# One written-out list of operations in a searched order, and query decays made once for both blocks

## The chip, the cores and the metric

The kernel runs on one core of one Trainium2 chip. The time is the device time of one execution in microseconds; lower is better. A profiled execution gives a trace beside it, whose span reaches from the first to the last instruction of the core. The engines are named as in the profile: PE (matrix products), PEld (its weight loads), DVE (vector), ACT (scalar activations), POOL (GpSimd) and SP, which here only issues transfers. Transfers are issued by SP, ACT and POOL and are called by the queue that issued them.

## What is computed

A decayed linear attention over `q`, `k`, `v` of 4 batches, 8 heads, 768 positions and 64 channels, and on its output a two-layer network with a leaky step:

```python
for b in range(nb):                       # blocks of the sequence
    intra = (qb @ kb.T * Dmask) @ vb      # Dmask = lam ** (i - j) below the diagonal
    inter = (qb * lam_pow) @ kv_state     # lam_pow = lam ** (i + 1)
    out[block] = intra + inter
    kv_state = lam ** block * kv_state + (kb * rev_pow).T @ vb
x = out as 3072 rows of 512
h = x @ w_in                              # 512 x 2048
g = max(h, 0) + alpha * min(h, 0)
result = g @ w_out                        # 2048 x 512
```

## The kernel before

The sequence is handled in blocks of 128, two of them (256 positions) at a time. The work is cut into 24 **units**; a unit is a chunk `c` of 0 to 5, one of two batches `bi` and one half `hh` of the heads. Four units give the 512 rows of one chunk, on which the network then runs.

For a unit `n` the steps are these. `load` and `load16` bring q, k, v; `load` uses SP and keeps 32 bits, `load16` uses POOL and casts to 16 bits in the transfer. `cast` (L268) copies q or k to 16 bits on the engine that its last argument names (A is ACT, V is DVE, G is POOL). `turn` (L288) transposes with PE into the PSUM bank "tk" and `turned` copies the result out; from unit 8 on `turn_by_dma` (L306) does the same with a transfer from SP. `key_decayed` (L278) and `decayed` (L315) multiply k and q by their decays. `cluster(old, new)` (L330) issues PE's products: first those of the old unit with the state (L346), then the scores of the new one (L364), the old unit's scores times v (L376) and the new unit's keys times v (L393). `masked` (L402) multiplies the scores by the decay mask on DVE, `state` (L419) advances the state `R`, `spread` (L439) copies it into the block-diagonal tile `RD`, and `out_of` (L407) copies the unit's output to `xT`.

For chunk `c` the network has 16 slices `f`. `up(c, f, bi, slot)` (L454) makes one 128 by 512 product in four matmuls, or half of it when `bi` is given, in the PSUM bank `slot`. `below` (L467) is ACT's relu of the negative, `gate` (L478) joins it on DVE into `g`. `down(c, t, part)` (L487) multiplies `g` by a quarter of `w_out`, `store` (L507) writes the rows out. For chunks 3 to 5 the second product is made by `product` (L582) in seven products instead of eight, from sums of blocks of `g` and `w_out` (`gate_sum`, `gate_copied`, `gate_added`, `weight_sum`); `taken` (L609) takes the results and writes them out.

`load_win(i)` and `load_wout(i)` (L109, L115) bring a quarter of each weight matrix, on POOL's queue. `fill` (L238) issues matmuls that nobody reads. `hold` (L83) writes one element of a raw tile on DVE, so that the load into that tile, which SP issues, cannot start before DVE has come to this point.

Nothing reorders the operations: the kernel runs under a manual schedule. Each engine does its instructions in the order in which the code calls them and waits for semaphores in between. Up to `key_decayed(18, "G")` (L661 to L1176) the calls are written out one by one; from there on loops produce them: `weave` (L1210) deals attention steps and network steps of chunks 3 and 4 alternately, and the last loop (L1261 to L1276) does the network of chunk 5.

The places that the prediction speaks of, in the order of the calls: `hold("k", 1, 0)` and the load of k for chunk 1, first batch; `cast(4, "k", "A")` (L759); `out_of(2, "A")` (L765) and `fill(14, 0)` (L767); `hold("k", 1, 1)` (L790) and the load of k for chunk 1, second batch; `load_wout(0)` to `load_wout(3)`; then

```python
    key_decayed(6, "G")        # L839, needs k of chunk 1, second batch
    key_decayed(7, "G")        # L840
...
    cast(6, "k", "G")          # L848
...
    turn(6)                    # L858
```

Of the kernel before, what the change touches and what calls it, by code (L numbers as in the profile page):

```python
# [11 lines left out]
def kernel(  # L12
# [132 lines left out]
    pos_i = const.tile([128, 2, 2, 64], int32, name="pos_i")  # L145
    pos_f = const.tile([128, W], fp32, name="pos_f")
# [6 lines left out]
    qdecay = const.tile([128, 2, 2, 2, L], fp32, name="qdecay")  # L153
# [9 lines left out]
    def positions():  # L163
        for half in range(2):
            nc.gpsimd.iota(
                rel_i[ds(half * 64, 64)], pattern=[[1, 3], [2, 64]], base=-1, channel_multiplier=-2
            )
        for half in range(2):
            nc.gpsimd.iota(
                rev_i[ds(half * 64, 64)], pattern=[[-1, 2]], base=L - 1, channel_multiplier=-2  # L170
            )
        nc.gpsimd.iota(pos_i, pattern=[[1, 2], [0, 2], [2, 64]], base=1, channel_multiplier=0)

    def zeros():
        for t in RD.values():
            nc.vector.memset(t, 0.0)
# [5 lines left out]
    def distances():  # L182
# [3 lines left out]
        nc.vector.tensor_copy(out=pos_f, in_=pos_i.rearrange("p e h j -> p (e h j)"))  # L186
# [14 lines left out]
    def decay_mask(hp):  # L201
        for hl in range(2):
            h = 2 * hp + hl
            nc.scalar.activation(dmask[:, hl, hp], rel_f, AF.Exp, scale=loglam[:, h : h + 1])  # L204

    def causal(hh):

        for hl in range(2):
            m = dmask[:, hl, ds(2 * hh, 2)]
            nc.vector.tensor_tensor(  # L210
                out=m, in0=m, in1=keep.unsqueeze(1).to_broadcast([128, 2, 3, 64]), op=ALU.mult
            )

    def key_decay():
        for e in range(2):
            nc.scalar.activation(kdecay[:, :, e], loglam, AF.Exp, scale=rev_f[:, e : e + 1])
# [4 lines left out]
    def query_decay(hp, block):  # L221
        x = qdecay[:, hp // 2, :, hp % 2, ds(block * 64, 64)]
        f = pos_f.rearrange("p (e a j) -> p e a j", e=2, a=2)[:, :, block]
        nc.scalar.activation(x, f, AF.Exp, scale=llp[:, hp : hp + 1])
# [90 lines left out]
    def decayed(n, eng="G"):  # L315
# [3 lines left out]
        p = ds(64, 64) if c < 2 else ds(0, L)  # L319
        engine(eng).tensor_tensor(  # L320
            out=qdT[:, :, :, p],
            in0=t["qkT"][:, 0, :, :, p],
            in1=qdecay[:, hh, :, :, p],
            op=ALU.mult,
# [231 lines left out]
    def parts(c, k, h, where="q"):  # L556

        if k != 3 and (c, k) not in SUM:
# [5 lines left out]
            2: lambda: (block_of(c, 0, 0, h), x[1]),  # L564
            3: lambda: (x[3], block_of(c, 0, 0, h)),
            4: lambda: (block_of(c, 0, 1, h), x[2]),
# [92 lines left out]


    positions()  # L661
    warm_up()
    load("q", 0, 0, 0)
    identity()
    load("k", 0, 0, 0)
    hold("k", 0, 1, 0)
    load16("v", 0, 0, 0)
    distances()
    load16("q", 0, 0, 1)
    logs()  # L670
    decay_mask(0)
    cast(0, "q", "A")
    key_decay()
    query_decay(0, 0)
    decay_mask(1)
    load16("v", 0, 0, 1)
    cast(0, "k", "G")
    load_alpha()
    fill(36, 2)
    turn(0)  # L680
    zeros()
    key_decayed(0, "V")
    load16("q", 0, 1)
    turned(0, "V")
    decay_mask(3)
    load("k", 0, 0, 1)
    load16("v", 0, 1)
    load_win(0)
    state_decay()
    decay_mask(2)  # L690
    query_decay(1, 1)
    fill(15, 2)
    cluster(None, 0)
    causal(0)
    load("k", 0, 1, 0)
    state(0, 0)
    hold("k", 2, 0)
    cast(1, "q", "A")
    cast(1, "k", "V")
    fill(17)  # L700
    spread(0, 1, "V", True)
    load16("v", 1, 0)
    query_decay(0, 1)
    fill(5, 2)
    turn(1)
    causal(1)
    cast(2, "q", "G")
    masked(0, 0)
    slopes(2)
    key_decayed(1, "V")  # L710
    decayed(0, "G")
    query_decay(3, 1)
    turned(1, "A")
    load("k", 0, 1, 1)
    cast(2, "k", "A")
    hold("k", 1, 0)
    masked(0, 1)
    fill(16, 2)
    turn(2)
    cluster(0, 1, True)  # L720
    query_decay(2, 1)
    state(0, 1)
    cast(3, "k", "A")
    decayed(1, "G")
    load16("q", 1, 0)
    load_win(1)
    masked(1, 1)
    cast(3, "q", "A")
    masked(1, 0)
    turned(2, "A")  # L730
    key_decayed(3, "G")
    spread(1, 1, "A", True)
    state(1, 0)
    spread(8, 0, "G")
    out_of(0, "V")
    fill(6, 2)
    cluster(1, None)
    key_decayed(2, "V")
    decayed(2, "G")
    load16("q", 1, 1)  # L740
# [3 lines left out]
    load_win(2)  # L744
    up(0, 0, 0, 2)
    turned(3, "A")
    state(2, 0)
    spread(2, 1, "A", True)
    below(0, 0, 0)
    masked(2, 0)  # L750
    load_win(3)
    state(1, 1)
    masked(2, 1)
    decayed(3, "G")
    gate(0, 0, 0)
    cluster(2, 3, True)
    load("k", 1, 0)
    up(0, 2, 0, 2)
    cast(4, "k", "A")  # L759
    key_decayed(4, "G")  # L760
    query_decay(3, 0)
    spread(3, 1, "A", True)
    masked(3, 0)
    state(3, 0)
    out_of(2, "A")  # L765
    state(2, 1)
    fill(14, 0)  # L767
    up(0, 1, 0, 0)
    state(3, 1)
    masked(3, 1)  # L770
    up(0, 3, 0, 1)
    below(0, 3, 0)
    cast(4, "q", "V")
    cluster(3, None)
    gate(0, 3, 0)
    turn(4)
    out_of(3, "A")
    below(0, 1, 0)
    below(0, 2, 0)
    gate(0, 1, 0)  # L780
    gate(0, 2, 0)
    load16("v", 1, 1)
    up(0, 6, None, 1)
    up(0, 2, 1, 0)
    cast(5, "k", "G")
    up(0, 5, None, 2)
    turned(4, "A")
    cluster(None, 4)
    below(0, 2, 1)
    hold("k", 1, 1)  # L790
    below(0, 6, None)
    below(0, 5, None)
    state(4, 0)
    gate(0, 2, 1)
    load_wout(0)
    load("k", 1, 1)
    key_decayed(5, "G")
    gate(0, 6, None)
    load_wout(1)
    up(0, 0, 1, 0)  # L800
    up(0, 4, None, 1)
    spread(10, 0, "G")
    cast(5, "q", "G")
    gate(0, 5, None)
    below(0, 0, 1)
    below(0, 4, None)
    up(0, 8, None, 2)
    decayed(4, "G")
    masked(4, 0)
    turn(5)  # L810
    load("k", 2, 0)
    state(4, 1)
    gate(0, 0, 1)
    spread(4, 1, "G")
    cast(7, "q", "G")
    up(0, 3, 1, 0)
    below(0, 8, None)
    spread(9, 0, "G")
    gate(0, 4, None)
    turned(5, "A")  # L820
    up(0, 7, None, 1)
    gate(0, 8, None)
    masked(4, 1)
    below(0, 3, 1)
    load("q", 2, 0)
    up(0, 1, 1, 2)
    cluster(4, 5)
    gate(0, 3, 1)
    decayed(5, "V")
    hold("k", 3, 0)  # L830
    below(0, 1, 1)
    load_wout(2)
    cast(6, "q", "G")
    up(0, 9, None, 0)
    below(0, 7, None)
    gate(0, 1, 1)
    up(0, 11, None, 2)
    state(5, 0)
    key_decayed(6, "G")  # L839
    key_decayed(7, "G")  # L840
    spread(5, 1, "A")
    masked(5, 1)
    out_of(4, "A")
    gate(0, 7, None)
    below(0, 9, None)
    below(0, 11, None)
    gate(0, 9, None)
    cast(6, "k", "G")  # L848
    gate(0, 11, None)
    up(0, 14, None, 1)  # L850
    query_decay(1, 0)
    up(0, 12, None, 0)
    state(5, 1)
    up(0, 10, None, 2)
    masked(5, 0)
    cast(7, "k", "G")
    below(0, 14, None)
    turn(6)  # L858
    cast(8, "k", "G")
    gate(0, 14, None)  # L860
    below(0, 12, None)
    gate(0, 12, None)
    cluster(5, None)
    below(0, 10, None)
    gate(0, 10, None)
    up(0, 15, None, 1)
    out_of(5, "A")
    turned(6, "V")
    up(1, 0, 0, 0)
    below(0, 15, None)  # L870
    load_wout(3)
    up(0, 13, None, 2)
    below(1, 0, 0)
    gate(0, 15, None)
    spread(11, 0, "A")
    cluster(None, 6)
    down(0, 2, 0, 1)
    turn(7)
    gate(1, 0, 0)
    below(0, 13, None)  # L880
    up(1, 2, 0, 0)
    gate(0, 13, None)
    state(6, 0)
    up(1, 1, 0, 2)
    state(6, 1)
    turned(7, "A")
    decayed(6, "G")
    masked(6, 1)
    masked(6, 0)
    spread(6, 1, "G")  # L890
    down(0, 2, 1, 2)
    below(1, 2, 0)
    cluster(6, 7)
    state(7, 0)
    gate(1, 2, 0)
    below(1, 1, 0)
    cast(8, "q", "A")
    gate(1, 1, 0)
    key_decayed(8, "G")
    down(0, 1, 0, 0)  # L900
    masked(7, 1)
    down(0, 1, 1, 2)
    down(0, 0, 0, 2)
    load16("v", 2, 0)
    spread(7, 1, "V")
    cast(9, "k", "V")
    down(0, 0, 1, 1)
    down(0, 2, 2, 2)
    down(0, 0, 2, 1)
    down(0, 2, 3, 2)  # L910
    hold("k", 2, 1)
    down(0, 0, 3, 1)
    cast(9, "q", "G")
    state(7, 1)
    out_of(6, "A")
    down(0, 1, 2, 2)
    masked(7, 0)
    turn_by_dma(8)
    decayed(8, "V")
    decayed(7, "G")  # L920
    load("k", 2, 1)
    cluster(7, 8)
    store(0, 0)
    masked(8, 1)
    up(1, 3, 0, 2)
    state(8, 0)
    query_decay(2, 0)
    down(0, 1, 3, 2)
    store(0, 2)
    turn_by_dma(9)  # L930
    spread(14, 0, "G")
    masked(8, 0)
    key_decayed(9, "G")
    out_of(7, "A")
    below(1, 3, 0)
    load("q", 2, 1)
    cast(10, "k", "V")
    up(1, 4, None, 1)
    gate(1, 3, 0)
    store(0, 1)  # L940
    up(1, 5, None, 0)
    state(8, 1)
    below(1, 4, None)
    up(1, 0, 1, 2)
    spread(8, 1, "G")
    gate(1, 4, None)
    load("q", 3, 0)
    below(1, 5, None)
    below(1, 0, 1)
    load("k", 3, 0)  # L950
    gate(1, 5, None)
    load16("v", 2, 1)
    cluster(8, 9)
    up(1, 1, 1, 1)
    cast(11, "k", "A")
    up(1, 6, None, 0)
    below(1, 1, 1)
    gate(1, 0, 1)
    key_decayed(10, "G")
# [347 lines left out]
```

## Time and profile before

| what | value |
|---|---|
| median of 3 timed runs | 220.3 us (220.16 to 220.39) |
| the profiled execution's own time | 221.63 us |
| its span | 219.8 us |
| mean granted PE clock over the span | 0.983 of full |
| transfers | 33.55 MB, 153 GB/s over the span |

The profile is read in this order. The busy shares say which engine has the least air; the 40 slices say when it has none; the windows give the same for stretches of one's own choice. The chain of waits goes back from the last instruction and names at each step what released it, so it says what a microsecond is worth where. The timeline of one engine shows each instruction with the idle time ahead of it. The view of the transfers has the time from issue to landing.

### The profile page before, as it was taken

What the parts mean: (1) busy time and instruction counts of PE and PEld (TensorE: products, weight loads), DVE (VectorE), ACT (ScalarE), POOL (GpSimd) and SP (SyncE); (2) the same over time, 40 slices, a digit from 0 to 9 for tenths busy, and PEclk for the clock granted to TensorE, in tenths of its full rate; (3) what the DMA queues carried; (4) which work ended last, traced back from release to release, by engine and by line L of the source; (5) the groups of instructions that cost most, each with busy time, mean ns of one, the idle gap of its engine ahead of it and who ended that gap; (6) DMA issues with size and microseconds to landing.
All of it is one profiled execution on the core that took longest, in us unless ns stands there. A gap on an engine that the chain in (4) does not pass through costs nothing.

```text
span 219.8 us, 5672 instructions
## 1 busy us (share of the span) xinstructions
PE 203.8 (93%) x2286; PEld 125.9 (57%) x2286; DVE 151.4 (69%) x306; ACT 117.0 (53%) x231; POOL 100.0 (46%) x162
## 2 busy tenths in 40 slices
PE   4877799399999999999999999999999999999993
PEld 4765556156455455454554555457667666666882
DVE  3899378736568874777897865875855577877811
ACT  3995488445164753447574644577445634445220
POOL 8769962448143944073558346759294100000000
PEclk9999799969999999999999999999999999999999
DMA  4999999954999999649899924797664220102123
GB/s 122 223 188 236 190 195 222 258 94 59 178 287 261 207 294 221 206 60 140 176 283 213 131 62 132 190 198 208 142 119 72 75 71 3 48 20 79 48 73 121
DMA packets 66027, 33.55 MB, mean 153 GB/s; under 512 B 34496, under 2 KB 62672, under 8 KB 66000
## 3 DMA queue, kind: packets, MB, share of 16 engines
q1 hardware_dynamic: 42576, 19.67, 37.4%
q0 software_dynamic: 21520, 10.36, 36.3%
q10 hardware_dynamic: 1904, 3.16, 4.1%
q8 instruction: 18, 0.29, 0.5%
q14 instruction: 9, 0.07, 0.1%
HBM read 27.28 MB, written 6.29 MB: 153 GB/s over the span
## 4 chain that ended last, share of the span: by engine, by line
PE 76%; DMA 11%; ACT 6%; DVE 3%; POOL 1%; issue 1%; ACTq 0%; POOLq 0%
PE h_ps L459 33%; PE o_ps L493 18%; PE p_ps L600 17%; DMA kraw<-in_k_dram 9%; PE s L364 3%; PE acc L376 2%; PE acc L346 2%; DMA lam_sb<-in_lam_dram 2%; ACT dmask L204 1%; PE acc L393 1%; POOL kdec L283 1%; ACT m L470 1%; DVE g L483 1%; ACT xT L252 1%; ACT RD L252 1%
## 5 line engine op out<-in xcount | busy, mean ns | idle before, releaser
L483 DVE SCALAR_TENSOR_TENSOR g<-m,oma,h_ps 128x512 f16<-128x512 f32 (+1 forms) x104 | 71.9, 704 | 40.4 <-ACT m L470 39.2
L459 PE MATMUL h_ps<-xT,w_in_sb 128*128 128x512 f16 (+1 forms) x416 | 97.7, 370 | 0.5 <-DVE g L483 0.5
L470 ACT ACTIVATE m<-h_ps 128x512 f32<-128x512 f32 (+1 forms) x104 | 57.9, 564 | 57.4 <-PE h_ps L459 54.2
L459 PEld LDWEIGHTS <-w_in_sb 128*128 128x128 f16 x416 | 40.1, 100 | 37.9 <-issue 3.0
L493 PE MATMUL o_ps<-w_out_sb,g 128*128 128x512 f16 x192 | 47.1, 379 | 0.0
L256 POOL COPY RD<-R 64x128 f16<-64x128 f16 x54 | 17.8, 330 | 48.4 <-DVE R L430 35.0
L405 DVE TENSOR_TENSOR sm<-s,dmask 128x512 f16<-128x512 f32 x48 | 31.8, 684 | 4.1 <-PE s L364 3.9
L493 PEld LDWEIGHTS <-g 128*128 128x128 f16 x192 | 18.2, 98 | 20.2
L283 POOL TENSOR_TENSOR kdec<-kraw,kdecay 128x512 f16<-128x512 f32 x21 | 21.9, 1048 | 8.4 <-DMA kraw<-in_k_dram 7.1
L600 PEld LDWEIGHTS <-g 128*128 128x128 f16 x192 | 18.7, 98 | 5.4
L320 POOL TENSOR_TENSOR qdT<-qkT,qdecay 128x512 f16<-128x512 f16 (+1 forms) x20 | 20.3, 1013 | 1.6 <-ACT qkT L252 0.5
L252 ACT ACTIVATE xT<-acc 128x512 f16<-128x512 f32 x20 | 11.9, 596 | 10.9 <-PE acc L376 4.9
L430 DVE SCALAR_TENSOR_TENSOR R<-R,rdecay,acc 128x64 f16<-128x64 f16 x60 | 13.9, 273 | 4.0 <-ACT xT L252 4.0
L600 PEld LDWEIGHTS <-gsum 128*128 128x128 f16 x144 | 14.1, 98 | 4.2
L242 PE MATMUL op_fill<-ident 128*128 128x128 f16 x109 | 9.1, 250 | 6.5 <-POOL ident masks.py:199 2.8
L624 ACT ACTIVATE o_sb<-p_ps 128x512 f32<-128x512 f32 (+1 forms) x16 | 7.9, 491 | 10.3 <-PE p_ps L600 10.3
L513 ACT ACTIVATE o_sb<-o_ps 128x512 f32<-128x512 f32 x12 | 7.1, 595 | 9.3 <-PE o_ps L493 9.3
L242 PEld LDWEIGHTS <-ident 128*128 128x128 f16 x109 | 8.1, 114 | 6.9 <-issue 3.9
L600 PE MATMUL p_ps<-w_out_sb,g 128*128 128x256 f16 x96 | 12.0, 273 | 0.0
L600 PE MATMUL p_ps<-wsum,gsum 128*128 128x256 f16 x96 | 12.0, 273 | 0.0
L600 PE MATMUL p_ps<-wsum,g 128*128 128x256 f16 x96 | 12.0, 273 | 0.0
L102 POOL DMA_DIRECT2D vh<-in_v_dram x13 | 11.8, 909 | 0.0
(84 smaller groups left out, 193.2 us busy)
## 6 DMA issues: line engine op xcount, KB each, us to landing
kraw<-in_k_dram SPq DMA_DIRECT2D x10, 512.0 KB, 7.9
qraw<-in_q_dram SPq DMA_DIRECT2D x8, 512.0 KB, 6.7
out_dram<-o_sb ACTq DMA_DIRECT2D x12, 256.0 KB, 5.7
out_dram<-o_sb SPq DMA_DIRECT2D x24, 128.0 KB, 2.0
vh<-in_v_dram POOLq DMA_DIRECT2D x11, 256.0 KB, 7.1
w_in_sb<-in_moe_w_in_dram POOLq DMA_DIRECT2D x4, 512.0 KB, 8.9
w_out_sb<-in_moe_w_out_dram POOLq DMA_DIRECT2D x4, 512.0 KB, 11.1
gsum<-g SPq DMA_DIRECT2D x6, 256.0 KB, 2.5
```

Of the source, the lines that this page charges most:

```text
L242: nc.tensor.matmul(t[:, 0:128], lhsT=ident, rhs=ident, start=True, stop=True)
L252: nc.scalar.activation(out, in_, AF.Copy)
L256: nc.gpsimd.tensor_copy(out=out, in_=in_)
L283: engine(eng).tensor_tensor(out=kdec, in0=kr, in1=d.unsqueeze(3).to_broadcast([128, 2, 4, D]), op=ALU.mult)
L320: engine(eng).tensor_tensor(out=qdT[:, :, :, p], in0=t["qkT"][:, 0, :, :, p], in1=qdecay[:, hh, :, :, p], op=ALU.mult,)
L405: nc.vector.tensor_tensor(out=t["sm"][hl], in0=t["s"][hl], in1=mask_of(hl, units[n][2]), op=ALU.mult)
L430: nc.vector.scalar_tensor_tensor(out=then[:, hp], in0=R[b, hh, i][:, hp], scalar=rdecay[:, 2 * hh + hp : 2 * hh + hp + 1], in1=kv[:, hp], ...
L459: nc.tensor.matmul(h_ps[:, 0:n] if bi is None else h_ps[:, 0:n].rearrange("p (e j) -> p e j", e=2), lhsT=w_in_sb[:, gi, ts(f, 128)], rhs=x ...
L470: nc.scalar.activation(m[:, 0:n], HP[c, f, bi][:, 0:n], AF.Relu, scale=-1.0)
L483: nc.vector.scalar_tensor_tensor(out=g, in0=mv, scalar=oma[:, f : f + 1], in1=hv, op0=ALU.mult, op1=ALU.add)
L493: nc.tensor.matmul(O[c, t], lhsT=gated(c, f)[:, t // 2, t % 2, :], rhs=w_out_sb[:, f, :], start=(f == 0), stop=(f == NF - 1),)
L600: nc.tensor.matmul(acc, lhsT=lhsT, rhs=rhs, start=(first and j == 0), stop=(j == NJ - 1), skip_group_check=True,)
```

## The change

The list of calls is replaced from the first to the last: what the loops made is written out too, and the order of everything is new. Of PE's instructions there are as many as before (4573 with weight loads and branches), of the same kinds. The helpers change so that a call is one instruction or a few (`zeros`, `decay_mask`, `causal`, `key_decay` take the piece as an argument), `load` may also be issued by POOL (`ring=1`), and the engine of many copies is another one. The decay of the queries is the same in both blocks of 64 positions of a row of `qdecay`; it was kept twice and made by eight activations, and is now kept once, made by four, and read with a repeated index.

```diff
-    def load(x, c, bi, part=None):
+    def load(x, c, bi, part=None, ring=0):
         h0, n = (0, H) if part is None else (part * H // 2, H // 2)
-        nc.sync.dma_start(
+        (nc.sync, nc.gpsimd)[ring].dma_start(
...
-    def zeros():
-        for t in RD.values():
-            nc.vector.memset(t, 0.0)
+    def zeros(b, hh, eng="V"):
+        engine(eng).memset(RD[b, hh], 0.0)
...
-    def query_decay(hp, block):
-        x = qdecay[:, hp // 2, :, hp % 2, ds(block * 64, 64)]
-        f = pos_f.rearrange("p (e a j) -> p e a j", e=2, a=2)[:, :, block]
-        nc.scalar.activation(x, f, AF.Exp, scale=llp[:, hp : hp + 1])
+    def query_decay(hp):
+        nc.scalar.activation(
+            qdecay[:, hp // 2, :, hp % 2, :], pos_f, AF.Exp, scale=llp[:, hp : hp + 1]
+        )
...
         engine(eng).tensor_tensor(
-            out=qdT[:, :, :, p],
-            in0=t["qkT"][:, 0, :, :, p],
-            in1=qdecay[:, hh, :, :, p],
-            op=ALU.mult,
+            out=x, in0=y, in1=d.unsqueeze(2).to_broadcast([128, 4, n, 64]), op=ALU.mult
         )
```

In the list, the parts around the places named above, as they stand after the change (other calls lie between them where three points stand):

```python
    decayed(0, "V")
    key_decayed(2, "G")
    hold("k", 1, 0)
...
    load("k", 1, 0)
...
    cast(5, "k", "G")
...
    load16("q", 1, 1)
...
    cast(4, "k", "G")
    key_decayed(4, "G")
...
    key_decayed(5, "G")
    load_win(3)
    out_of(2, "A")
    fill(14, 0)
...
    cast(4, "q", "A")
...
    hold("k", 1, 1)
...
    decayed(5, "G")
...
    load_wout(0)
    up(0, 11, None, 2)
    cast(6, "q", "G")
    load_wout(1)
    cast(6, "k", "G")
...
    key_decayed(6, "G")
...
    load_wout(2)
    spread(5, 1, "G")
...
    load_wout(3)
    turn(6)
...
    key_decayed(7, "G")
```

Further on, q of chunks 3 and 4 and k of chunks 3 and 4 (six of the loads) go through POOL:

```python
    load("q", 3, 0, ring=1)
...
    cast(12, "q", "G")
...
    load("q", 4, 1, ring=1)
    load("k", 3, 1, ring=1)
    load("k", 4, 0, ring=1)
...
    load("k", 4, 1, ring=1)
...
    load("q", 4, 0, ring=1)
```

And the last lines, where before the results of the seventh product were taken right behind it for each batch:

```python
    product(5, 3, 0, None, True)
    taken(5, 3, 0)
    taken(5, 4, 1)
    taken(5, 3, 1)
```

More of the change, by code (lines that the diff above doesn't have):

```diff
@@ L721 @@
[L721 to L725, printed above, removed]
[L726 to L740 removed]
+    cluster(None, 0)
+    causal(0, 1)
+    load("k", 0, 1, 1)
+    key_decayed(1, "V")
@@ L827 @@
     cluster(4, 5)
[L828 to L831, printed above, removed]
-    load_wout(2)
[L833 to L849, printed above, removed]
+    up(0, 9, None, 0)
```

1236 lines of the change are left out of this document (771 added, 465 removed).

## The prediction

> **What bounds the kernel now.** I read the span first, then the windows of my own choice, then the chain of waits, and last the timelines around the places where the chain leaves PE.
>
> ```profile
> span 219.8 us, 5672 instructions
> ...
> 0.00:44.15 44.15, 32.49 (x513) 23.22 (x513) 31.63 (x79) 30.24 (x70) 30.77 (x54) 0.96 1.25 204
> 44.15:203.07 158.92, 158.18 (x1656) 91.17 (x1657) 112.98 (x215) 83.07 (x152) 69.23 (x109) 0.99 0.71 146
> 203.07:219.80 16.73, 13.10 (x120) 11.49 (x118) 6.74 (x13) 3.67 (x9) 0.00 (x0) 0.98 0.24 79
> ```
>
> The columns of a window are its length, the busy time of PE, PEld, DVE, ACT and POOL, the granted PE clock, the share of the transfers and GB/s. From 44.15 to 203.07 us PE is busy for 158.18 of 158.92 us: no order can take more than the 0.74 us of gaps and what the clock held back. In the first 44.15 us PE is busy for 32.49 us, and some of that is fill or half speed; there the transfers are saturated (share 1.25). The tail is PE too. So the prediction is made ahead of 44.15 us, and the rest asks only whether the new order keeps PE full.
>
> The chain of waits (start, length, what):
>
> ```profile
> 14.46 7.00 DMA kraw<-in_k_dram
> ...
> 21.56 0.63 ACT qk L252
> ...
> 23.22 0.28 ACT xT L252
> ...
> 23.55 0.96 PE op_fill L242 x14
> ...
> 24.54 1.87 PE h_ps L459 x8
> ...
> 29.07 12.25 DMA kraw<-in_k_dram
> ...
> 41.49 2.05 POOL kdec L283 x2
> 43.54 0.56 POOL qk L256
> ...
> 44.15 0.62 PE tp L295 x8
> ...
> 45.39 3.74 PE h_ps L459 x12
> ...
> 203.07 13.11 PE p_ps L600 x120
> 216.20 0.42 DVE o_sb L622
> ```
>
> It leaves PE twice for a load of k. The first one, k of chunk 1, first batch, is held until 14.46 us and lands at 21.5; ACT stands at the cast of it, and behind that in ACT's queue is the copy to `xT` that frees the bank of the next `up`. The second, k of chunk 1, second batch, is held until 29.07, lands at 41.35, and then POOL makes both decayed keys (2.05 us) ahead of the cast (0.56) that `turn(6)` needs.
>
> PE's timeline around the second gap, its line at 27.91, and the clock in four windows of 1 us:
>
> ```profile
> 27.91 2.33 PE L459 MATMUL h_ps<-xT,w_in_sb 128*128 128x512 f16 x12
> 39.00 1.89 PE L459 MATMUL h_ps<-xT,w_in_sb 128*128 128x512 f16 x8 [0.23 <-DVE g L483]
> 44.15 0.62 PE L295 MATMUL tp<-ident,qk 128*128 128x128 f16 x8 [3.26 <-POOL qk L256]
> 25.00:26.00 1.00, 1.00 (x7) 0.67 (x6) 0.22 (x1) 0.00 (x0) 0.98 (x3) 0.50 1.30 203
> ...
> 45.00:46.00 1.00, 1.00 (x18) 0.43 (x11) 0.50 (x1) 0.57 (x1) 1.00 (x2) 0.50 0.10 31
> ...
> 47.00:48.00 1.00, 1.00 (x6) 0.75 (x5) 0.12 (x1) 0.60 (x1) 0.00 (x0) 0.50 0.84 62
> ```
>
> PE ends its work at 40.89 and idles 3.26 us. After either gap the granted clock is 0.50: the twelve matmuls at 45.39 take 3.74 us, where at full clock (1.89 for eight, with 0.16 of overlap, so 0.22 each) they take 2.6.
>
> **The change part by part.** PE's order up to `turn(6)` is the old one but for swaps of neighbours, so what comes ahead of it is decided by the other queues.
>
> *Start.* `hold("k",1,0)` now comes in DVE's queue ahead of a mask and both first `masked`; counting DVE's queue through, I put it at 12.3 us (estimate). With the 7.0 us of the load it lands at 19.3. Its cast (unit 4) goes to POOL, so ACT reaches the `xT` copy without it: about 21.9, after `cluster(2,3)` at 20.5, and the first `up` behind the fill starts at 23.0, where it was 24.54. Then ACT stands at `cast(4,"q")` instead, whose q POOL issues at about 15.6 and which lands 7.4 later, at 23.0. What is late next is ACT's copy of unit 3 and the gate that frees bank 1: the first whole `up` (27.91 before) starts at about 26.0. **-1.9 us**; bounds 0 (ACT's new wait is as long as the old) and -3.3 (both waits gone).
>
> The transfers that this and the next step rest on, issue to landing, from views narrowed to one load (k at 14.46, k at 29.07, 16-bit q, q at 30.1, then the parts of `w_out` in order, the last of them alone in flight):
>
> ```profile
> kraw<-in_k_dram SPq DMA_DIRECT2D x1, 512.0 KB, 7.0
> kraw<-in_k_dram SPq DMA_DIRECT2D x1, 512.0 KB, 12.2
> qh<-in_q_dram POOLq DMA_DIRECT2D x1, 256.0 KB, 7.4
> qraw<-in_q_dram SPq DMA_DIRECT2D x1, 512.0 KB, 16.0
> w_out_sb<-in_moe_w_out_dram POOLq DMA_DIRECT2D x1, 512.0 KB, 11.4
> w_out_sb<-in_moe_w_out_dram POOLq DMA_DIRECT2D x1, 512.0 KB, 13.3
> ...
> w_out_sb<-in_moe_w_out_dram POOLq DMA_DIRECT2D x1, 512.0 KB, 5.9
> ```
>
> *The gap at 40.89.* `hold("k",1,1)` comes three DVE operations later in the list but the work ahead of it runs 1.9 us earlier, so the load starts at 29.0 as before. In flight beside it before were two parts of `w_out`; now there is the end of `w_in`, and `w_out` starts only at about 33. I take 8 us, nearer the 7.0 than the 12.2: it lands at 37. Its cast stands ahead of the decayed keys, not behind (0.56 us): 37.6. PE comes to `turn(6)` at 26.0 plus the 12.98 us that lie between 27.91 and 40.89, at 39.0. The wait is covered; **-3.26**. With 12.2 us it would be 41.8, and 2.8 of it come back.
>
> *The clock.* Without the gap the half clock from 45.0 to 48.3 goes: **-1.65**. Here the Trainium skill says more (TensorE: Matmul & The Clock Gate, section What's actually happening): a PE idle for about one window of 3.4 us falls to half clock and stays there for about as long. The second gap (3.26 idle, 3.3 at half) agrees; the first one was filled for its last microsecond (the fill at 23.55) and was halved too. By the rule alone short new waits cost only themselves; by the rows they may cost the 1.65 again. The sum takes no second halving.
>
> *w_out later.* POOL issues the first part behind `decayed(5)`, which waits for `turn(5)` and ACT's copy: about 33.2 instead of 25.0. The first `down` is due 4.05 us of PE work after `turn(6)`, at 43.05. With the 11.4 us of the row it lands at 44.6, with 5.9 at 39: **+1.0**, bounds 0 and +3.4 (13.3).
>
> *POOL's queue in the same stretch.* Durations of POOL and of what moves to DVE and off ACT:
>
> ```profile
> L283 POOL TENSOR_TENSOR kdec<-kraw,kdecay 128x512 f16<-128x512 f32 x21 | 21.9, 1048 | 8.4 <-DMA kraw<-in_k_dram 7.1
> ...
> L256 POOL COPY RD<-R 64x128 f16<-64x128 f16 x54 | 17.8, 330 | 48.4 <-DVE R L430 35.0
> ...
> L320 POOL TENSOR_TENSOR qdT<-qkT,qdecay 128x512 f16<-128x512 f16 (+1 forms) x20 | 20.3, 1013 | 1.6 <-ACT qkT L252 0.5
> ...
> L256 POOL CAST qk<-kraw 128x512 f16<-128x512 f32 x13 | 7.9, 612 | 4.9 <-ACT qk L252 3.6 <-DMA kraw<-in_k_dram 0.9
> ...
> L102 POOL DMA_DIRECT2D vh<-in_v_dram x13 | 11.8, 909 | 0.0
> L283 DVE TENSOR_TENSOR kdec<-kraw,kdecay 128x512 f16<-128x512 f32 x3 | 2.5, 847 | 0.1
> ...
> L254 DVE COPY RD<-R 64x128 f16<-64x128 f16 x4 | 1.4, 347 | 0.0
> ...
> L254 DVE CAST xT<-acc 128x512 f16<-128x512 f32 x2 | 1.4, 688 | 0.1
> L224 ACT ACTIVATE qdecay<-pos_f,llp 128x128 f32<-128x128 f32 x8 | 3.0, 391 | 0.5 <-ACT o_sb L513 0.5
> ```
>
> From the landing of k at 37 POOL has, up to `key_decayed(7)` that `cluster(6,7)` needs: three decayed keys at 1.05, five casts at 0.61, three issues at 0.91, two pairs of `RD` copies at 0.66 and one decayed q at about 0.7, 11.0 us, so 48.0. PE is there at 39.0 plus 9.24 of work and about 1 us of waits, 49; but `cast(8,"q")` in that queue waits for a load that took 16.0. **+0.5**, bounds 0 and +2.
>
> *Moved work and query decays.* DVE gets six more decayed keys, eight more pairs of `RD` copies and six more `xT` copies: 6 x 0.85 + 8 x 0.69 + 6 x 0.69 = 14.8 us. Its cover is DVE's idle time, 46 us of the 159; if that is gone at a place, PE waits up to 0.7 there. Four `qdecay` activations go (4 x 0.39 = 1.6 us of ACT); three of the eight ran after 22 us under ACT's idle, and all four kept ones run in the start: nothing. The repeated index in `decayed` is not in the trace; the decayed keys read `kdecay` in that manner at 1.05 us against 1.0 for `decayed`, so nothing, at most 0.05 each under POOL's idle.
>
> *End.* DVE takes two results behind the last product, not one, and SP's last three stores follow: 0.42 x 1 = **+0.4**, bounds 0 and +0.7.
>
> Sum: -1.9 - 3.26 - 1.65 + 1.0 + 0.5 + 0.4 = -4.9; span 219.8 to 214.9. The profiled execution's own time is 221.63, 1.33 above the median of the runs, 220.3; I take the 4.9 from the median: **215.4 us**.
>
> **The rivals.** *More is won.* If `w_out` and POOL are in time and the first half clock (24.7 to 27.5, 1.4 us) goes too: -4.9 - 1.0 - 0.5 - 1.4 = -7.8, 212.5. For it: fewer bytes are in flight beside each load that PE awaits. Against: the bytes are the same and the transfers were saturated.
>
> *The gap only moves.* The same bytes must land, and the late `w_out` takes 13.3: PE waits 3.45 at the first `down` instead of 1.0, and the clock is halved again (1.65): -4.9 + 2.45 + 1.65 = -0.8, 219.5. For it: the share of 1.25 over the whole first window. Against: the last `w_out` took 5.9 alone.
>
> *POOL blocks on its own loads: slower.*
>
> ```profile
> qraw<-in_q_dram SPq DMA_DIRECT2D x8, 512.0 KB, 6.7
> ...
> vh<-in_v_dram POOLq DMA_DIRECT2D x11, 256.0 KB, 7.1
> ```
>
> Six loads leave SP for POOL, and `cast(12,"q")` stands on POOL behind the issue of its own load with four operations between. Until it lands POOL does nothing; behind it, up to `decayed(11)`, are eight issues, four casts, two decayed keys, three decayed q's and a pair of copies: 7.3 + 2.4 + 2.1 + 3.1 + 0.7 = 15.6 us. Between `cluster(7,8)` and `cluster(11,12)` PE has 25 whole parts of 0.865, five halves and three clusters of about 1 us, 26.8 us; the load is issued some 2 us into it. Slack is 26.8 - 2 - 15.6 = 9.2 less the landing. With 6.7 or 7.1 it fits; with 16.0 PE waits 6.8: 222.2. It makes the change a loss from a landing of 14.1 on. A page of the Trainium skill, SBUF — State Buffer, section SBUF: two separate sides, speaks for this one: vector work in some modes keeps GpSimd from writing descriptors, and loads of SP are free of that. The rows of before, 909 ns for an issue, show no such delay here; no run here shows it for these loads.
>
> **How the numbers follow.** Forecast 215.4, chance 0.48; more won, 0.20; the gap moves, 0.16; POOL blocks, 0.16. The range goes from the first rival with half a microsecond to spare, 211.9, over the second, to 220.4; it leaves out the third. A measurement tells 0.2% (0.44 us) from no change: faster 0.48 + 0.20 + most of the second, 0.79; within 0.2%, 0.04; slower 0.17.
>
> **What would show it.** PE at the eight transposes of `turn(6)` near 39 us without a gap of over 1 us; no window at clock 0.50 after 30 us; the k load of 29.0 landed by 38; a wait at the first `down` of about 1 us; and from there PE over 99% busy. Wrong it is if PE idles for over 2 us between 40 and 55, or POOL has a wait of over 4 us for a load after 55 with PE waiting for `qdT`.

## The result, and the profile after

The changed kernel takes **228.15 us** (median of 4 executions, 227.53 to 229.33), beside 220.34 us of the kernel before on the same chip: 1.0349 times as long, 95% interval 1.0294 to 1.0404. The forecast was 215.4 us, the range 211.9 to 220.4: wrong, and on the wrong side. Ratios here and below leave out executions over 1.5% above the fastest of the same kernel; where these are many (e1, e6, e9, e13, e14, e16), the median and the range of all tell more than the ratio.

The profiled execution took 228.05 us. Two lines of its page, then lines of PE's timeline up to its longest wait:

```profile
span 225.8 us, 5654 instructions
...
PE 202.2 (90%) x2286; PEld 125.8 (56%) x2286; DVE 165.9 (73%) x332; ACT 108.0 (48%) x219; POOL 97.5 (43%) x150
```

```profile
26.53 2.33 PE L457 MATMUL h_ps<-xT,w_in_sb 128*128 128x512 f16 x12
...
39.23 0.61 PE L291 MATMUL tp<-ident,qk 128*128 128x128 f16 x8
...
43.43 1.03 PE L491 MATMUL o_ps<-w_out_sb,g 128*128 128x512 f16 x4
...
48.94 1.02 PE L491 MATMUL o_ps<-w_out_sb,g 128*128 128x512 f16 x4 [1.02 <-DVE g L481]
...
69.30 2.75 PE L457 MATMUL h_ps<-xT,w_in_sb 128*128 128x512 f16 x12 [1.37 <-DVE g L481]
...
77.67 0.39 PE L344 MATMUL acc<-qdT,RD 128*128 128x128 f16 x4
86.19 0.64 PE L362 MATMUL s<-qkT 64*64 64x128 f16 x16 [8.13 <-DMA qkT<-qk]
```

The first part came nearly at the forecast times: the first whole `up` at 26.53 (forecast 26.0), `turn(6)` at 39.23 with no wait, the first `down` at 43.43. In `cluster(10, 11)` PE then stands for 8.13 us, because the transpose of unit 11 has not landed. The windows around it (columns as in the prediction) show the second part of the price:

```profile
30.00:44.15 14.15, 14.15 (x184) 8.56 (x182) 12.78 (x24) 9.85 (x21) 11.35 (x20) 1.00 1.19 235
...
80.00:82.00 2.00, 0.00 (x0) 0.00 (x0) 0.00 (x0) 0.00 (x0) 0.61 (x1) 0.65 0.95 252
82.00:84.00 2.00, 0.00 (x0) 0.00 (x0) 0.00 (x0) 0.00 (x0) 0.00 (x0) 0.50 1.49 165
...
88.00:90.00 2.00, 2.00 (x8) 0.82 (x6) 2.00 (x5) 0.88 (x3) 0.25 (x1) 0.50 1.63 118
90.00:92.00 2.00, 2.00 (x9) 0.86 (x8) 1.16 (x3) 0.00 (x0) 0.91 (x2) 0.79 1.46 187
...
94.00:220.00 126.00, 126.00 (x1267) 77.91 (x1264) 97.48 (x182) 59.57 (x110) 33.83 (x51) 1.00 0.48 106
```

PE's clock falls to half in the wait and is whole again at about 90.8 (0.79 over 90 to 92). From 86.2 to 90.8 PE works at half speed: 4.6 us, 2.3 of them lost (the expectations below have 2.65, a coarser reading). 8.1 + 2.3 = 10.4, and 225.8 - 10.4 = 215.4, within half a microsecond of the forecast span of 214.9 (the terms ahead of it do not all agree, as shown below). From 94 us PE is again busy throughout.

SP's timeline in four narrow windows has the transposes of units 12, 13, 11 and 14 in the order of issue; the view of the transfers, narrowed to the third, has its time from issue to landing:

```profile
64.84 1.81 SPq L305 DMA_TRANSPOSE qkT<-qk  x1
...
68.73 1.43 SPq L305 DMA_TRANSPOSE qkT<-qk  x1
...
70.32 4.25 SPq L305 DMA_TRANSPOSE qkT<-qk  x1
...
81.22 1.31 SPq L305 DMA_TRANSPOSE qkT<-qk  x1
```

```profile
qkT<-qk SPq DMA_TRANSPOSE x1, 15.8
```

Unit 11 is needed first and is third in line. POOL's timeline shows what is issued meanwhile:

```profile
64.77 0.60 POOL L252 CAST qk<-kraw 128x512 f16<-128x512 f32 x1
...
68.03 1.04 POOL L89 DMA_DIRECT2D qraw<-in_q_dram  x1
69.07 1.78 POOL L89 DMA_DIRECT2D kraw<-in_k_dram  x2
...
71.84 0.92 POOL L89 DMA_DIRECT2D kraw<-in_k_dram  x1
...
74.38 0.89 POOL L102 DMA_DIRECT2D vh<-in_v_dram  x1
75.26 0.89 POOL L89 DMA_DIRECT2D qraw<-in_q_dram  x1
76.14 0.90 POOL L102 DMA_DIRECT2D vh<-in_v_dram  x1
...
77.64 0.88 POOL L102 DMA_DIRECT2D vh<-in_v_dram  x1
```

The cast of k for unit 11 ends at 65.4: its transpose could go then, 5 us earlier (in e1 below it goes at 65.95). And five loads of 512 KB and three of v are issued within 10 us, with the transposes in flight.

### The profile page after: what moved, and what is told of

Same layout as the page of the kernel before. It is cut to its first block, busy times and chain, and to the rows that moved or that the text cites. A ratio compares the mean times of both kernels' runs of the same rounds, so it can differ in the third digit from the quotient of the medians.

```text
span 225.8 us, 5654 instructions
## 1 busy us (share of the span) xinstructions
PE 202.2 (90%) x2286; PEld 125.8 (56%) x2286; DVE 165.9 (73%) x332; ACT 108.0 (48%) x219; POOL 97.5 (43%) x150
## 4 chain that ended last, share of the span: by engine, by line
PE 73%; DVE 9%; DMA 9%; ACT 5%; issue 2%; DVEq 0%; ACTq 0%
PE h_ps L457 32%; PE p_ps L598 16%; PE o_ps L491 16%; DMA qkT<-qk 7%; PE s L362 3%; PE acc L374 2%; DVE g L481 2%; DVE RD L250 2%; DMA lam_sb<-in_lam_dram 2%; PE acc L344 2%; PE acc L391 1%; DVE dmask L207 1%; ACT qkT L248 1%; ACT RD L248 1%; DVE sm L403 1%
## 5 line engine op out<-in xcount | busy, mean ns | idle before, releaser
L457 PE MATMUL h_ps<-xT,w_in_sb 128*128 128x512 f16 (+1 forms) x416 | 92.9, 364 | 1.7 <-DVE g L481 1.7
L481 DVE SCALAR_TENSOR_TENSOR g<-m,oma,h_ps 128x512 f16<-128x512 f32 (+1 forms) x104 | 71.1, 702 | 21.4 <-ACT m L468 20.0
L468 ACT ACTIVATE m<-h_ps 128x512 f32<-128x512 f32 (+1 forms) x104 | 56.8, 564 | 60.9 <-PE h_ps L457 59.2
L457 PEld LDWEIGHTS <-w_in_sb 128*128 128x128 f16 x416 | 39.3, 98 | 38.7 <-issue 1.9
L491 PEld LDWEIGHTS <-g 128*128 128x128 f16 x192 | 18.7, 100 | 23.1 <-issue 3.0
L598 PEld LDWEIGHTS <-g 128*128 128x128 f16 x192 | 18.8, 98 | 4.8
L252 POOL COPY RD<-R 64x128 f16<-64x128 f16 x34 | 10.1, 298 | 24.6 <-DVE R L428 18.4
L362 PE MATMUL s<-qkT 64*64 64x128 f16 x384 | 10.3, 226 | 10.9 <-DMA qkT<-qk 8.1
L279 POOL TENSOR_TENSOR kdec<-kraw,kdecay 128x512 f16<-128x512 f32 x15 | 16.2, 1085 | 0.2
L511 ACT ACTIVATE o_sb<-o_ps 128x512 f32<-128x512 f32 x12 | 7.1, 595 | 17.0 <-PE o_ps L491 16.6
L362 PEld LDWEIGHTS <-qkT 64*64 64x64 f16 x384 | 6.3, 108 | 13.7 <-DMA qkT<-qk 8.3
L248 ACT ACTIVATE xT<-acc 128x512 f16<-128x512 f32 x14 | 8.3, 596 | 11.4 <-PE acc L391 6.7
L598 PE MATMUL p_ps<-wsum,gsum 128*128 128x256 f16 x96 | 12.3, 273 | 0.0
```

Source lines behind the costliest of these rows:

```text
L248: nc.scalar.activation(out, in_, AF.Copy)
L252: nc.gpsimd.tensor_copy(out=out, in_=in_)
L279: engine(eng).tensor_tensor(out=kdec, in0=kr, in1=d.unsqueeze(3).to_broadcast([128, 2, 4, D]), op=ALU.mult)
L362: nc.tensor.matmul(s[hl][ds(a * 64, 64), hp, 1 - e, :].rearrange("p (e j) -> p e j", e=2), lhsT=t["qkT"][p, 1, e, hp, ds(a * 64, 64)], rhs ...
L457: nc.tensor.matmul(h_ps[:, 0:n] if bi is None else h_ps[:, 0:n].rearrange("p (e j) -> p e j", e=2), lhsT=w_in_sb[:, gi, ts(f, 128)], rhs=x ...
L468: nc.scalar.activation(m[:, 0:n], HP[c, f, bi][:, 0:n], AF.Relu, scale=-1.0)
```

## The experiments

"Unit 11's transpose" is `turn_by_dma(11)`, "v of chunk 3" `load16("v", 3, 0)` and `(3, 1)`.

| run | edit | median, range of all (us) | ratio to before, interval |
|---|---|---|---|
| e1 | after, unit 11's transpose first | 222.29, 217.40 to 232.99 | 0.993, 0.9885 to 0.9974 |
| e2 | after, six loads on SP | 228.77, 227.73 to 232.10 | 1.0363, 1.0312 to 1.0414 |
| e3 | after, loads of chunk 4 later | 223.77, 221.79 to 226.13 | 1.0125, 1.0072 to 1.0179 |
| e4 | start of after, rest of before | **216.85**, 216.60 to 217.15 | **0.9824**, 0.9793 to 0.9856 |
| e5 | start of before, rest of after | 234.54, 233.61 to 244.64 | 1.0607, 1.0554 to 1.0661 |
| e6 | e1 and e3 together | 224.13, 219.10 to 226.83 | 0.9974, 0.9926 to 1.0023 |
| e7 | before, gap alone | 217.36, 216.42 to 217.53 | 0.9835, 0.9802 to 0.9868 |
| e8 | before, query decays once | 221.00, 219.15 to 221.63 | 0.9994, 0.9952 to 1.0036 |
| e9 | after, transfers in before's order | 223.68, 220.22 to 227.69 | 1.0037, 0.998 to 1.0095 |
| e10 | e4, six loads on POOL | 219.31, 217.41 to 220.87 | 0.9874, 0.9818 to 0.9931 |
| e13 | e1, and v of chunk 3 first | 221.68, 217.37 to 226.78 | 0.9871, 0.9802 to 0.9941 |
| e14 | after, v of chunk 3 first | 226.99, 220.31 to 236.89 | 1.0016, 0.9966 to 1.0066 |
| e15 | e13, six loads on SP by need | 220.48, 217.54 to 222.31 | 0.9935, 0.9895 to 0.9974 |
| e16 | e13, three loads later | 224.12, 218.97 to 226.91 | none: one left |

**The halves of the list (e4, e5).** Both lists hold the same calls (the helpers of the start are those of after in both), so they can be cut at `spread(7, 1)` and joined crosswise.

> The list of the changed kernel from its first call to spread(7, 1) (about 52 us), and from there on every remaining call in the order, on the engine and on the queue of the kernel before. The prediction's sum (start 1.9, gap 3.26, clock 1.65, less 1.0 and 0.5) says 220.3 - 5.3 = 215.0 us, if the loss is all behind 52 us. Rival: the new order of the start takes something away from the rest (buffers and loads that come earlier or later), so that the loss comes with it: 220 us or more.

> The list of the kernel before up to spread(7, 1) (about 58 us), then the remaining calls in the order, on the engines and on the queues of the changed kernel. If the start's gain and the later loss are independent: 220.5 + 228.2 - 216.9 = 231.8 us, with a wait of PE of some 8 us for the transpose of unit 11. Rival (the loss comes of the earlier start, which brings the loads of weights and the later ones closer together): 220 to 223 us.

The start of after with the rest of before wins 1.8%, and its executions lie within 0.55 us; by the medians it wins 4.1 us, where its expectation had 5.3, so it is partly luck that its profiled span is 214.9 us, the span that the prediction summed. The other way round the kernel loses 6.1%, some 3 us more than the 231.8 of two independent parts; in its profile, of its longest execution (244.64), PE waits 18.75 us for unit 11's transpose, which took 26.6 to land. So the loss comes with the rest of the list and the gain with the start. The two do not quite add up, and what makes up the 3 us is not shown.

**The gain by itself (e7, e8).**

```diff
-    load_wout(0)          # ahead of load("k", 1, 1)
-    load_wout(1)
...
+    load_wout(0)
+    load_wout(1)
     load_wout(2)
...
+    cast(6, "k", "G")
     key_decayed(6, "G")
     key_decayed(7, "G")
...
-    cast(6, "k", "G")
```

> The kernel before with two edits: the first two parts of w_out are issued just ahead of the third, and the cast of k for unit 6 stands on POOL ahead of the decayed keys of 6 and 7. By the prediction's terms: the load issued at 29.07 lands at about 37 instead of 41.3, the wait of 3.26 us and the half clock behind it (1.65) go, w_out is in time because the start is not earlier: 220.5 - 4.9 = 215.6 us. Rival (the load took 12.2 us for its own place among loads that stay): it lands after 40, 1 to 2.5 us are won, 218 to 219.5 us.

> The kernel before with the decay of the queries kept once: four activations of the eight, and the repeated index in the decayed queries; the order is otherwise the old one. By the prediction nothing: 220.5 us, within 0.3. Rival: an ACT operation of 0.39 us less ahead of the first units brings the start forward, up to 0.4 us won; or the repeated index costs 0.05 us and more on each of the 23 decayed queries, 221 us.

e7 gives 0.9835, 3.6 us by the medians, of the 4.9 expected. The transfers of the window 28.5 to 29.5, and PE's timeline:

```profile
kraw<-in_k_dram SPq DMA_DIRECT2D x1, 512.0 KB, 5.5
```

```profile
40.66 0.61 PE L295 MATMUL tp<-ident,qk 128*128 128x128 f16 x8
...
44.40 1.04 PE L493 MATMUL o_ps<-w_out_sb,g 128*128 128x512 f16 x4
```

The load that took 12.2 us takes 5.5 without the two parts of `w_out` beside it; `turn(6)` is at 40.66 without a gap, and the first `down` at 44.40, where before it was at 49.53. Of the start's gain beyond the gap little is left in the end: e4 is 0.0011 below e7, within the intervals. e8 shows no effect of the part of the change that its name tells of, as forecast.

**Order or bytes (e1, e2, e3).**

```diff
+    turn_by_dma(11)       # e1
     turn_by_dma(12)
...
-    load("q", 4, 1, ring=1)    # e2: the six without ring=1
+    load("q", 4, 1)
...
     cast(14, "k", "G")
+    load("q", 4, 1, ring=1)    # e3: moved here from 68 to 78 us
+    load("k", 4, 0, ring=1)
+    load("k", 4, 1, ring=1)
+    load("q", 4, 0, ring=1)
+    load16("v", 4, 0)
```

> One transfer moves: the transpose of unit 11 stands on SP ahead of that of unit 12, not behind that of 13. Theory O (order: unit 11's transpose is issued at 70.3 us although its operands are ready at 65.4, and comes in the thick of the loads): issued at about 65.5 it lands in 5 to 6 us, by 72, the 8.13 us wait of PE at 78.06 and the half clock behind it (2.65) go, 228.15 - 10.8 = 217.4 us, or 215.5 if nothing else is late. Theory C (contention: the loads that POOL issues from 68 to 78 us slow every transpose, wherever it stands): unit 11 is out of it, but those of 12, 13 and 14 land later instead; PE gets a wait of 3 to 6 us at the scores of unit 12, 13 or 14, 221 to 225 us.

> The six loads of q and k of chunks 3 and 4 that POOL issues are issued by SP at the same places of the list; nothing else changes. Theory P (what hurts is that POOL's queue issues them): the transposes land in 3 to 5 us as in the kernel before, the 8.13 us wait goes, 216 to 219 us. Theory C (the bytes in flight hurt, whoever issues them) : the transposes of 11, 13 and 14 still take 10 us or more, or stand on SP behind loads that wait for a free buffer; the wait of PE stays at 5 to 10 us, 225 to 231 us. Theory O says the same as C here.

> Five loads (q and k of chunk 4, 512 KB each, and v of chunk 4, first batch) stand on POOL behind the cast of k for unit 14, some 10 us later; the order of the transposes on SP stays as it is in the changed kernel. Theory C: with only one load of k and two of v beside them the transposes of 13, 11 and 14 land in 4 to 6 us each; unit 11 lands by 77 us, the 8.13 us wait and its half clock go, about 217.4 us; the loads that come later cost at most a wait of 2 us behind 95 us. Theory O: unit 11 is still issued at 70 us or later behind unit 13's transpose, the wait stays at over 4 us, 223 us or more.

Each theory got half of what it asked. e1: issued at 65.95, the transpose lands in 4.4 us, the wait is gone, and the profiled execution takes 217.4 us; but six of the other eleven take 224 to 233. e3: with the old place in line but fewer loads beside it, it lands in 7.2 us and PE does not wait for it; instead POOL stands 9.32 us at a cast of q whose load it issued late, and PE 2.75 us for a decayed q. e2: on SP the loads stand in one line with the transposes, unit 11's is issued only at 77.1 and lands in 9.7 us, and PE waits 10.4.

**What comes back in e1's longer executions (two more traces of it, e11 and e12).**

> The kernel with unit 11's transpose first once more, for a trace of one of its longer executions (its times went from 217.4 to 233.0 us). If it comes out over 223 us: a wait of PE of 5 us or more, and by the theory of the bytes in flight it is for the transpose of unit 13 or 14, or for a decayed q that POOL makes behind one of them; by a theory of the order alone it would be again for unit 11. If it comes out below 221 us it tells nothing new.

> The same kernel a third time, for the same reason and with the same expectations: over 223 us with a wait of PE of 5 us or more behind the transpose of unit 13 or 14 (bytes in flight) or of unit 11 (order alone); below 221 us it tells nothing new.

e11 took 220.38 us, e12 228.72. Neither side of the expectation was right: in e12 PE waits neither for 11 nor for 13 or 14. PE's timeline, POOL's, and the landing of that load:

```profile
94.58 0.43 PE L391 MATMUL acc<-vh,kdec 64*64 64x64 f16 x16 [8.35 <-DMA vh<-in_v_dram]
```

```profile
75.23 0.89 POOL L102 DMA_DIRECT2D vh<-in_v_dram  x1
```

```profile
vh<-in_v_dram POOLq DMA_DIRECT2D x1, 256.0 KB, 19.3
```

It is v of chunk 3, issued behind four loads of q and k, three of them of chunk 4. The stretch 60 to 82 us in the shorter (profiled e1) and the longer execution (e12) of this one kernel:

```profile
60.00:82.00 22.00, 21.60 (x251) 11.76 (x249) 20.71 (x42) 11.82 (x24) 17.83 (x23) 1.00 1.17 258
```

```profile
60.00:82.00 22.00, 20.44 (x244) 11.18 (x243) 20.71 (x41) 11.68 (x24) 17.55 (x23) 1.00 1.12 190
```

The engines of the transfers are as busy (1.17 and 1.12), but they moved 258 GB/s in one and 190 in the other.

**One cure after the other (e6, e9, e13 to e16).** e6 has the edits of e1 and e3 and moves `cast(17, ...)` and `turn_by_dma(17)` behind `turn_by_dma(16)`; e9 leaves the engines in after's order and gives SP the order of before. The others, against after:

```diff
+    turn_by_dma(11)            # e13, e15, e16
     turn_by_dma(12)
...
+    load16("v", 3, 0)          # e13 to e16
+    load16("v", 3, 1)
...
     turn_by_dma(13)
+    load("q", 4, 0)            # e15: the six on SP, four of them here
+    load("k", 4, 0)
+    load("q", 4, 1)
+    load("k", 4, 1)
...
     cast(17, "k", "G")
+    load("q", 4, 1, ring=1)    # e16: moved here
+    load("k", 4, 1, ring=1)
+    load16("v", 4, 0)
```

> Both cures in the changed kernel: the transpose of unit 11 ahead of that of 12, and the five loads of chunk 4 on POOL behind the cast of k for unit 14; besides, the casts and the transpose of unit 17 stand behind the transpose of unit 16, so that POOL does not stand at a cast of 17 while its load is in flight (9.32 us with the loads later alone). Theory (order and bytes in flight together are the whole loss): no wait of PE over 1 us behind 45 us, 215 to 217.5 us, and the single executions lie within 2 us of one another. Rival (the new order of the engines has further waits of its own behind 80 us): a wait of over 2 us at another place, 219 us or more.

> The list of the changed kernel, with PE, DVE, ACT and POOL in its order, but behind spread(7, 1) SP issues the 28 loads and transposes in the order of the kernel before (the six loads of POOL among them on SP), each as early in the list as its operands allow. Theory X (only the order of the transfers costs): the wait of 8.13 us at unit 11 goes and no other comes, 216.9 us as with the first part alone, at most 218. Theory Y (the new order of the four engines behind 52 us costs by itself, because an engine's operation now stands ahead of what PE needs): a wait of over 2 us stays, 220 us or more.

> The changed kernel with two transfers moved: unit 11's transpose on SP ahead of unit 12's, and v of chunk 3 (both batches) on POOL ahead of the loads of q for chunk 4 and k for chunks 3 and 4. Theory L (the loss is just two transfers that are needed first and issued behind others needed later): no wait of PE over 1.5 us behind 45 us in any execution, 216.5 to 218 us, the single executions within 2 us of one another. Theory C (the bytes in flight slow whatever comes next): a third transfer is late, the times stay spread over 5 us or more, median 219 us or more.

> The changed kernel with v of chunk 3 on POOL ahead of the loads of q for chunk 4 and k for chunks 3 and 4; the transposes stay in their order. Theory L: unit 11's transpose is late as before, with 6 to 9 us of waiting in PE, 225 to 229 us. If the wait goes too (218 us or less), the place of the transpose on SP was not the cause, and the four loads ahead of it were.

> The changed kernel with the six loads of q and k on SP in the order of need: behind the transpose of unit 10 q of chunk 3, then the transposes of 11 and 12, k of chunk 3, the transpose of 13, and only then the four loads of chunk 4; v of chunk 3 stands on POOL where the burst began. Theory of the pace (SP issues in line, so the transposes that PE needs next are never behind six loads): no wait of PE over 1.5 us behind 45 us in any execution, 216.5 to 218 us, single executions within 2 us. Theory of the bytes alone (the same 3 MB between 63 and 82 us are in flight, whoever issues them): spread of 5 us or more, median 219 us or more.

> The changed kernel with unit 11's transpose ahead of unit 12's, v of chunk 3 ahead of the loads on POOL, and three loads (q and k of chunk 4, second batch, and v of chunk 4, first batch: 1.25 of the 3.25 MB that POOL asks for from 68 to 78 us) some 15 us later on POOL, behind the cast of k for unit 17. Theory D (density: as many bytes in that stretch as in the fast kernel, 2.25 MB from 68 to 79 us, and what is needed first issued first, are enough): 216.5 to 218.5 us, single executions within 2 us. Rival (the changed order has too little room behind 63 us for any load to be slower than usual, wherever the bytes are): a wait of over 2 us for some other transfer, median 219.5 us or more, spread over 4 us.

No edit brings the changed order to e4's time in every execution. In each profile another wait stands last: in e9 DVE at `cast(12, "k", "V")`, which its order has ahead of a gate, for a load that SP now issues later (PE 4.59 us); in e13 and e16 a stop of PE in the middle of a product (below); in e15 a decayed q (2.63 us) behind the transpose of unit 14, which SP issues only at 88.69, behind the loads; in e6 a copy to `RD` (1.67 us). e14 keeps the wait for unit 11 in its profile (2.67 us). Theory L, two misplaced transfers, fails with e13; theory D, the density, with e16: 1.25 MB less in the stretch, and k of chunk 3, second batch, still needs 16.6 us.

**The issuing queue (e10).**

```diff
-    load("q", 3, 0)
+    load("q", 3, 0, ring=1)    # and the other five, in e4
```

> The kernel with the changed kernel's first part and the old order behind it (216.85 us), but the six loads that the change gives to POOL are issued by POOL, at their places in that old order. If the path through POOL costs nothing but POOL's time for the issues (six of 0.92 us): 216.9 us, at most 217.5. If POOL as the issuer is harmful by itself (its queue in order: a load waits for its buffer and everything behind it on POOL waits too): a wait of PE for a decayed q or k of 2 us or more, 219 us or more.

e10 lies between the theories: 219.31 us, and behind 50 us not one long wait but several short ones (1.48 and less). From 60 to 82 us, the window and the transposes in it, first of e4 and then of e10:

```profile
60.00:82.00 22.00, 22.00 (x250) 11.73 (x249) 16.89 (x36) 11.10 (x21) 12.26 (x15) 1.00 1.26 247
```

```profile
qkT<-qk SPq DMA_TRANSPOSE x4, 5.7
```

```profile
60.00:82.00 22.00, 20.52 (x241) 10.83 (x240) 18.73 (x35) 10.54 (x20) 14.55 (x17) 1.00 1.28 181
```

```profile
qkT<-qk SPq DMA_TRANSPOSE x4, 11.1
```

With only the queue of six loads changed, the transfers' share stays (1.26, 1.28), the bytes per second fall from 247 to 181, and the four transposes take 11.1 us instead of 5.7 (medians). The queue changes the times of the loads too: POOL comes to three loads of chunk 4 at 77.4 to 81.4 us, which SP issued at 69.2 to 71.7, so part of the fall in bytes is that fewer were asked for. The first three transposes lie ahead of that difference and are issued within 0.8 us of each other in the two kernels; they land in 6.1, 5.4 and 6.2 us in e4, and in 11.7, 10.5 and 13.3 in e10.

The queue changes the packets as well. The lines of the two queues in the pages of e4 and then e10 (packets, MB, share; q1 is SP's queue, q0 POOL's):

```profile
q1 hardware_dynamic: 42576, 19.67, 39.4%
q0 software_dynamic: 21520, 10.36, 37.4%
```

```profile
q1 hardware_dynamic: 36336, 16.52, 37.8%
q0 software_dynamic: 22384, 13.50, 44.3%
```

By the differences the six loads are 6240 packets on SP and 864 on POOL, for the same 3.1 MB: about 500 bytes each there, 3.6 KB here.

That the queue by itself doubles the landing is not shown. There is one trace of each kernel, and the landing varies by more than that between executions of a single one: the transpose that e1 issues at 69.34 us, with POOL's loads beside it, landed in 7.7 us there, and the same one in 20.0 in e12 (issued at 69.50). What stands is that the six executions of e10 spread over 3.5 us, those of e4 over 0.55; the ratios, 0.9874 and 0.9824, have intervals that overlap.

## Why the prediction was wrong

**The start, -1.9.** It gave -1.4 (26.53 for 27.91), and not by the step that the prediction names. The load of k was not earlier: it was issued at 14.68 us, not at 12.3 (before 14.46), and the first `up` behind the fill began at 24.63, not at 23.0 (before 24.54). From there to the first whole `up` PE has the same work in both, 3.37 us before and 1.90 now. Ahead of the fill it idled 0.63 us instead of 2.24, and the granted clock stayed at 1.00, where before it was 0.50 from 25 to 27 us. So what was won is the first half clock, which the prediction had left to its first rival (1.4); that the size came near is luck. In e4, with the same calls, the `up` behind the fill began at 25.60, and the start gave 0.4.

**The gap, -3.26, and the clock, -1.65.** Right in mechanism, and shown alone by e7, where the medians give 3.6 of the 4.9. The load was issued at 30.06, not 29.0, and landed in 5.5 us (5.5 in e7, 5.6 in e4), not 8.

**w_out, +1.0.** It did not come: the first `down` started at 43.43 with no wait. A wait of the same size came later, at 48.94, for DVE.

**POOL's queue, +0.5.** Nothing there: `cluster(6, 7)` had no wait.

**Moved work, nothing.** A wait "up to 0.7" was allowed. DVE's copies of `RD` took up to 1.19 us each, not 0.35, as the chain of waits of after shows, and the `up` behind them came 1.37 us late:

```profile
65.98 0.95 DVE RD L250
...
66.95 1.19 DVE RD L250
...
69.30 1.02 PE h_ps L457 x4
70.32 15.82 DMA qkT<-qk
```

**The query decays, nothing.** Right (e8).

**The end, +0.4.** About +0.8: PE's products ended at 221.36 in a span of 225.8, 4.4 us ahead of its end; before it was 216.18 of 219.8, 3.6.

```profile
219.45 1.91 PE L598 MATMUL p_ps<-w_out_sb,gsum 128*128 128x256 f16 x16
```

**The step that failed** is the first one: "So the prediction is made ahead of 44.15 us, and the rest asks only whether the new order keeps PE full." That question was then put to POOL's queue alone. SP's queue was not walked, so it was not seen that units 12 and 13 had been put ahead of 11; and the forecast priced every load as in the kernel before (6.7 and 7.1 us; 16.0 only in a rival), though the list puts eight of them within 10 us, with two transposes among them. The three of v took 16.5 (median), unit 11's transpose 15.8. A busy PE in the old profile says what the old order achieves behind 44 us and nothing of the room of the new one.

The third rival had the mechanism nearest to it (a landing of over 14.1 us makes the change a loss), but at the wrong load: q of chunk 3 landed in 6.6 us and POOL lost 2.51 there. Long stops of POOL at a cast of its own load came in e3 (9.32 us), e12 (14.70) and e16 (8.81); only in e3 did PE then wait for a decayed q. A slip in the range changes nothing: half a microsecond below 212.5 is 212.0, not 211.9.

What is shown: the loss is behind 52 us (e4, e5); in the changed kernel it is unit 11's transpose and the half clock behind it (8.1 + 2.3); its place in line and the loads beside it each suffice to remove that wait (e1, e3); moved alone, it leaves others. What two queues do to each other stays in part open (e4, e10). The Trainium skill (DMA: Bandwidth & Descriptors, section Queues, rings and completion order) says that each of the 16 engines takes turns between the queues that have work, a packet at a time, so a transpose that has SP's line to itself still shares every engine when POOL has loads out. The doubling from 5.7 to 11.1 us in e10 agrees with sharing, as far as one trace can tell; turns of one packet each do not show: in e10 from 67 to 72 us, 54 packets of POOL's queue (0.21 MB) and 575 of SP's (0.15 MB) took nearly the same time of the engines, 59.6% and 57.3%. The fall of the total to 181 GB/s is not explained by it. In the line of one queue (e2, e15) a transpose waits behind loads instead.

The Trainium skill (SBUF — State Buffer, section SBUF: two separate sides) has another cause to offer, vector work that keeps POOL from writing descriptors. In e12 DVE and POOL are idle through nearly all of the wait (86.2 to 94.6 us), and the load still does not come:

```profile
88.00:90.00 2.00, 0.00 (x0) 0.00 (x0) 0.00 (x0) 0.00 (x0) 0.00 (x0) 1.00 0.88 116
90.00:92.00 2.00, 0.00 (x0) 0.00 (x0) 0.00 (x0) 0.00 (x0) 0.00 (x0) 0.70 1.67 150
92.00:94.00 2.00, 0.00 (x0) 0.00 (x0) 0.00 (x0) 0.00 (x0) 0.00 (x0) 0.50 1.11 164
```

So that is not what holds the load in this stretch.

**Open** stays why one kernel moves 258 GB/s in one execution and 190 in the next, at nearly the same share (1.17 and 1.12). Most versions with the changed order behind 63 us vary by several per cent. The old order of that stretch did not (216.60 to 217.15 in e4), and e4 and e7 are the fastest versions measured.

## What to carry to other kernels

When an order is changed, walk every queue that issues transfers, and for each transfer set its issue, a landing from the most crowded row and the time at which it is needed side by side; a landing measured where few bytes were out is no price for a stretch where many are. A transfer that is needed soon belongs ahead of loads that are needed late; in e13 and e15 that alone did not bring the time back. Moving loads to another queue is a change of its own, in the times of issue, the packets and the spread of the executions (e10), and deserves a run of its own. To tell a gain from a loss in one rewritten list, cut it where both lists have done the same calls and join the halves crosswise: two runs here said where to look.

## What the runs showed of the hardware

**The clock falls after short idle times, but not always.** In e16 PE idles 2.26 us (79.57 to 81.83), and the next windows are at half clock until about 85.4, 3.4 us:

```profile
82.00:83.00 1.00, 1.00 (x5) 0.52 (x4) 1.00 (x3) 0.42 (x2) 0.00 (x0) 0.50 0.67 209
...
85.00:86.00 1.00, 1.00 (x5) 0.37 (x4) 0.00 (x0) 0.00 (x0) 0.00 (x0) 0.82 0.75 205
```

The same followed 2.94 us in e13 and 2.75 in e3, but nothing followed 2.67 in e14 or 2.63 in e15. So an idle time of 2.3 to 2.9 us costs itself and, in three of these five cases, some 1.7 us more. The Trainium skill (TensorE: Matmul & The Clock Gate, section What's actually happening) gives an idle window of about 3.4 us as the condition, in a window that runs freely; here less was enough, and what decided is not shown. Ahead of 28 us it is the same: half clock followed 2.12 us in e7, 2.24 in the kernel before and 2.49 in e4, but not 2.78 in the kernel after.

**PE stopped in the middle of a product, with nothing to wait for that the profile shows**, at the same instruction in e13 and e16: one matmul of four, then 2.94 us (e13) or 2.26 us in which not even a weight load was issued. e13, PE's timeline, and the transfers of the window 77 to 79.2, just ahead of it:

```profile
78.96 0.27 PE L457 MATMUL h_ps<-xT,w_in_sb 128*128 128x256 f16 x1
82.17 0.49 PE L457 MATMUL h_ps<-xT,w_in_sb 128*128 128x256 f16 x3 [2.94 <-issue]
```

```profile
q0 software_dynamic: 55, 0.21, 86.7%
q8 instruction: 1, 0.02, 10.5%
```

A queue named "instruction" moved one packet of 0.02 MB there, among engines that were taken up by the loads. That PE waited for its own code is a guess from this, not shown: such packets also move where PE does not stop (three in e4 from 60 to 82 us).
